# w_in's second piece as one transfer of 512 KB on SP's queue instead of two of 256 KB

## Chip, core and metric

The kernel runs on one core of a Trainium2 chip. The metric is the device time of one execution in microseconds. TensorE (PE) multiplies, with its weight loads listed apart (PEld); VectorE (DVE), ScalarE (ACT) and GpSimd (POOL) do the elementwise work; SP only issues transfers. SP and ScalarE each have a queue of transfers, and both queues are served by the same 16 DMA engines.

## What is computed

One input x (2048 rows of 512, bf16) goes through two mixers, and a gate per row mixes their outputs:

```python
g = _sigmoid((x * gate_w).sum(-1, keepdims=True))
a = _A_ref(x, A_wqkv, A_w_phi, A_wo)       # linear attention, 32 heads of 16
b = _B_ref(x, B_w_in, B_w_sp, B_b_sp, B_w_out)
return g * a + (1 - g) * b
```

The change lies in the loads of the second mixer's first weight, `B_w_in` (512 x 1376):

```python
z = _gelu(jnp.einsum('bsd,df->bsf', x, w_in))
z1 = z[..., :Fh].copy()
z2 = _layernorm(z[..., Fh:], axis=-1)
g = jnp.einsum('ts,bsf->btf', w_sp, z2) + b_sp[None, :, None]
return jnp.einsum('bsf,fd->bsd', z1 * g, w_out)
```

## The kernel before

The 2048 rows are 16 tiles of 128. Everything stays in SBUF; the order of the instructions on each engine is the order in which the program writes them, and a framework adds the semaphores. First comes z = x w_in for all tiles, with the projections for the attention woven in from tile 5 on, then the keys together with the spatial product with w_sp, then the queries and the output.

The tile `w_in` holds the weight as [128 partitions, 4 blocks of 128 rows (dt), 1376 + 1 columns]; the last column is the gate's weight, put there by a small matmul (line 209) and a copy on VectorE (line 212). The product of a tile t with it is made in three pieces of columns, `Z_PIECES`: 0 to 511, 512 to 1023 and 1024 to 1376. A piece is one matmul for each dt (line 180), added up in PSUM; then ScalarE takes the GELU (line 215).

Tiles 0 and 1 are treated apart, because the weight is still arriving. Their x comes as rows (`xn`) and is transposed by TensorE, which first spins on a constant (line 189). The first piece is cut into two halves of 256 columns, and within a piece the two tiles alternate, dt by dt. For the second piece that means eight matmuls in the order dt 0 tile 0, dt 0 tile 1, dt 1 tile 0 and so on. The third piece follows tile by tile, and after tile 1 comes tile 2 with all its pieces, which reads the first transposed load of x (`xT`, line 123).

The loads of the beginning are issued in this order. On SP's queue: rows 0 to 127 of x (128 KB), blocks 0 and 1 of the first piece's two halves (two of 128 KB), the second piece as blocks 0 and 1, then 2 and 3 (two of 256 KB, lines 118 and 119), the third piece (352 KB, line 122), the transposed load of tiles 2 and 3 (line 123), wv (512 KB, line 124), and then further transposed loads. On ScalarE's queue: rows 128 to 255 of x, blocks 2 and 3 of the first piece's halves (two of 128 KB), and the gate's weight.

The framework has eight completion semaphores for such transfers and hands them out in turn, over both queues. A transfer that gets a semaphore for the second time waits, on the queue that issues it, until the transfer that had it first has landed. The second half of the second piece is the ninth transfer in that count; it takes the semaphore of the load of x on ScalarE's queue. The copy of line 212 writes a column of `w_in` and waits for the transfers of the columns about it, the third piece's among them.

Of the kernel before, what the change touches and what calls it, by code (L numbers as in the profile page):

```python
# [23 lines left out]
NDT = D // P  # L24
CH = 512
# [14 lines left out]
def kernel(  # L40
# [14 lines left out]
    nc = tc.nc  # L55
# [55 lines left out]
    def load_w_in(eng, d0, d1, n0, n1):  # L111
        eng.dma_start(out=w_in[:, d0:d1, n0:n1], in_=w_in_v[:, d0:d1, n0:n1])

    HC = CH // 2
    for n0 in (0, HC):
        load_w_in(nc.sync, 0, 2, n0, n0 + HC)
        load_w_in(nc.scalar, 2, 4, n0, n0 + HC)
    for d0 in (0, 2):
        load_w_in(nc.sync, d0, d0 + 2, CH, 2 * CH)
    nc.scalar.dma_start(out=gw[:], in_=gate_w.rearrange("(dt p) -> dt p", p=P))  # L120
    nc.scalar.activation(out=st[:, 9, 0:1], in_=ones[:, 0:1], func=AF.Gelu_apprx_tanh)
    nc.sync.dma_start(out=w_in[:, :, 2 * CH:F], in_=w_in_v[:, :, 2 * CH:F])
# [451 lines left out]
```

## Time and profile before

| | us |
|---|---|
| median of 3 runs (lowest to highest) | 208.38 (208.34 to 208.63) |
| the profiled execution's own time | 208.87 |
| its span, first to last instruction | 207.1 |
| TensorE busy | 202.6 (98% of the span) |
| VectorE busy | 148.5 (72%) |
| ScalarE busy | 82.1 (40%) |
| GpSimd busy | 49.5 (24%) |

The profile is one execution of the program. Each engine's busy time is the time in which it had an instruction in work; matmuls overlap in the pipeline, so the eight 128x512 matmuls of a piece are listed with some 0.38 us each and start 0.22 us apart. The granted clock of TensorE is 1.0 throughout. A transfer has two times: that of its issue on the queue, and the time from the start of the issue to the landing, at which its semaphore is complete. The 16 DMA engines moved 26.5 MB in all, 128 GB/s over the span; in the first four of the span's 40 slices (5.2 us each) it was 188, 233, 188 and 255.

### The profile page before, as it was taken

To read this page: it belongs to the slowest core of one execution; us is meant where nothing else is said; L and a number is where in the kernel's file an instruction comes from. 1 tells how busy PE (TensorE), PEld (TensorE's weight loads), DVE (VectorE), ACT (ScalarE), POOL (GpSimd) and SP (SyncE) were. 2 spreads that over 40 slices of the span, in tenths; PEclk is the share of its full clock that TensorE was granted. 3 is DMA by queue.
4 is the path that set the end of the run, shared out by engine and by line. 5 is a ranking of instruction groups with operands and counts; after the bars stand their busy time and mean duration, and the time that the engine had idled before them with its cause. 6 is when DMAs were issued, how large, how long until landed. Compare 5 with 4: busy or idle time off the path is not lost.

```text
span 207.1 us, 3685 instructions
## 1 busy us (share of the span) xinstructions
PE 202.6 (98%) x1399; PEld 118.2 (57%) x1399; DVE 148.5 (72%) x304; ACT 82.1 (40%) x145; POOL 49.5 (24%) x46
## 2 busy tenths in 40 slices
PE   8899999999999999999999999999999999999994
PEld 7454555555455666666666667666455555555543
DVE  1048858376887988878888996698989778795500
ACT  3266757575684424250505102222524243341122
POOL 4000000000002343525352544032522252322000
DMA  6999899997000634472757771137765963567451
GB/s 188 233 188 255 178 178 227 173 188 234 0 3 0 138 69 112 101 127 67 162 118 112 139 170 41 38 90 76 170 140 119 151 162 80 134 135 164 101 104 51
DMA packets 90378, 26.50 MB, mean 128 GB/s; under 512 B 84168, under 2 KB 90360, under 8 KB 90360
## 3 DMA queue, kind: packets, MB, share of 16 engines
q1 hardware_dynamic: 87360, 23.84, 58.9%
q10 hardware_dynamic: 3000, 2.43, 3.9%
q8 instruction: 11, 0.18, 0.4%
q14 instruction: 7, 0.06, 0.1%
HBM read 3.44 MB, written 2.10 MB: 27 GB/s over the span
## 4 chain that ended last, share of the span: by engine, by line
PE 98%; issue 0%; ACT 0%; DVE 0%
PE ps L396 36%; PE ps L180 18%; PE ps L327 13%; PE ps L439 10%; PE ps L444 7%; PE ps L282 7%; PE ps L420 2%; PE ps L372 2%; PE ps L189 1%; PE ps L305 1%; PE ps L195 0%; ACT ob L448 0%; DVE w_in L212 0%; PE ps L209 0%
## 5 line engine op out<-in xcount | busy, mean ns | idle before, releaser
L396 PE MATMUL ps<-zz,wsp 128*128 128x344 bf16 x512 | 79.1, 310 | 0.0
L342 POOL TENSOR_TENSOR w_in<-w_in,rs 128x512 bf16<-128x512 bf16 x28 | 41.3, 1475 | 124.8 <-DVE rs L340 117.3
L396 PEld LDWEIGHTS <-wsp 128*128 128x128 bf16 x512 | 49.9, 98 | 27.9
L333 ACT ACTIVATE w_in<-ps 128x512 bf16<-128x512 f32 x56 | 30.1, 596 | 63.5 <-issue 21.5
L180 PE MATMUL ps<-w_in,xT 128*128 128x512 bf16 (+2 forms) x200 | 39.8, 350 | 0.7 <-DVE w_in L212 0.7
L338 DVE TENSOR_REDUCE zs<-w_in 128x64 f32<-128x1024 bf16 x28 | 33.8, 1209 | 0.0
L404 DVE SCALAR_TENSOR_TENSOR u<-ps,bcol,zz 128x344 bf16<-128x344 f32 x32 | 18.4, 574 | 18.6 <-PE ps L396 18.5
L180 PEld LDWEIGHTS <-xT 128*128 128x128 bf16 x200 | 18.9, 97 | 18.5 <-DMA w_in<-in_B_w_in_dram 1.0
L215 ACT ACTIVATE zz<-ps 128x1376 bf16<-128x1376 f32 (+2 forms) x18 | 21.4, 1190 | 18.9 <-PE ps L180 18.8
L439 PE MATMUL ps<-w_out,uT 128*128 128x512 bf16 (+1 forms) x102 | 23.5, 367 | 0.0
L224 DVE BATCH_NORM_STATS2 stats<-zz 128x6 f32<-128x344 bf16 x32 | 14.8, 505 | 11.2 <-ACT zz L215 11.2
L342 DVE TENSOR_TENSOR w_in<-w_in,rs 128x512 bf16<-128x512 bf16 x28 | 19.4, 692 | 1.0
L340 DVE RECIPROCAL rs<-zs 128x64 f32<-128x64 f32 x32 | 17.7, 552 | 3.2
L448 ACT ACTIVATE ob<-ps 128x512 bf16<-128x512 f32 (+1 forms) x17 | 9.7, 572 | 25.2 <-PE ps L444 23.7
L444 PE MATMUL ps<-wo,oT 128*128 128x512 bf16 (+1 forms) x68 | 16.6, 367 | 0.0
L327 PE MATMUL ps<-wq,xT 128*128 128x512 bf16 x64 | 16.4, 379 | 0.0
L327 PE MATMUL ps<-wk,xT 128*128 128x512 bf16 x64 | 16.2, 379 | 0.0
L327 PEld LDWEIGHTS <-xT 128*128 128x128 bf16 x128 | 10.8, 97 | 9.0
L282 PE MATMUL ps<-wv,xT 128*128 128x512 bf16 x64 | 15.6, 380 | 0.0
L439 PEld LDWEIGHTS <-uT 128*128 128x128 bf16 x102 | 9.7, 98 | 10.0
L426 DVE SCALAR_TENSOR_TENSOR o<-ps,st,rd 128x512 bf16<-128x512 f32 x16 | 12.0, 751 | 0.6
L444 PEld LDWEIGHTS <-oT 128*128 128x128 bf16 x68 | 6.7, 98 | 7.2
(56 smaller groups left out, 119.2 us busy)
## 6 DMA issues: line engine op xcount, KB each, us to landing
out_dram<-ob ACTq DMA_DIRECT2D x15, 128.0 KB, 1.9
w_out<-in_B_w_out_dram SPq DMA_DIRECT2D x1, 640.0 KB, 5.0
w_in<-in_B_w_in_dram SPq DMA_DIRECT2D x2, 256.0 KB, 4.1
wv<-in_A_wqkv_dram SPq DMA_DIRECT2D x1, 512.0 KB, 5.0
wo<-in_A_wo_dram SPq DMA_DIRECT2D x1, 512.0 KB, 5.4
w_in<-in_B_w_in_dram SPq DMA_DIRECT2D x1, 352.0 KB, 5.2
w_in<-in_B_w_in_dram ACTq DMA_DIRECT2D x2, 128.0 KB, 3.9
w_in<-in_B_w_in_dram SPq DMA_DIRECT2D x2, 128.0 KB, 3.5
```

The lines of the kernel that those rows point to most:

```text
L180: nc.tensor.matmul(zb[:, n0:n1], lhsT=xT[:, dt, t * P:(t + 1) * P], rhs=w_in[:, dt, n0:n1], start=(dt == 0), stop=(dt == NDT - 1),)
L215: nc.scalar.activation(out=zz[:, t, n0:n1], in_=zbank(t)[:, n0:n1], func=AF.Gelu_apprx_tanh)
L282: nc.tensor.matmul(ps[:, b, :], lhsT=xT[:, dt, t * P:(t + 1) * P], rhs=wv[:, dt, :], start=(dt == 0), stop=(dt == NDT - 1),)
L327: nc.tensor.matmul(ps[:, b, :], lhsT=xT[:, dt, t * P:(t + 1) * P], rhs=w[:, dt, :], start=(dt == 0), stop=(dt == NDT - 1),)
L333: nc.scalar.activation(out=e[:, :, a, :], in_=src, func=AF.Exp, scale=sc)
L338: nc.vector.tensor_reduce(out=zs[:], in_=ev, axis=AX.X, op=ALU.add)
L340: nc.vector.reciprocal(out=rs[:], in_=zs[:])
L342: eng.tensor_tensor(out=ev[:, sl, :], in0=ev[:, sl, :], in1=rs[:, sl, None].to_broadcast([P, H, DH]), op=ALU.mult,)
L396: nc.tensor.matmul(ps[:, b, 0:HF], lhsT=wsp[:, tt % WSLOTS, s, :], rhs=zz[:, s, FH + h * HF:FH + (h + 1) * HF], start=(s == 0), stop=(s == ...
L404: nc.vector.scalar_tensor_tensor(out=u[:, h * HF:(h + 1) * HF], in0=ps[:, b, 0:HF], scalar=bcol[:, tt:tt + 1], in1=zz[:, tt, h * HF:(h + 1 ...
L439: nc.tensor.matmul(ps[:, b, n0:n1], lhsT=uT[:, ft, :], rhs=w_out[:, ft, n0:n1], start=(ft == 0), stop=False,)
L444: nc.tensor.matmul(ps[:, b, n0:n1], lhsT=oT[:, g, :], rhs=wo[:, g, n0:n1], start=False, stop=(g == NDT - 1),)
```

## The change

The two transfers of the second piece, each with two of the four blocks, become one with all four. It brings the same bytes to the same place, with rows of 1024 bytes as before; the matmuls that read them are the same. There is one transfer less in the program, so each later one gets the semaphore before the one it had: the 512 KB are the eighth transfer, and the third piece is now the ninth. Every line number below moves up by one.

```diff
     for n0 in (0, HC):
         load_w_in(nc.sync, 0, 2, n0, n0 + HC)
         load_w_in(nc.scalar, 2, 4, n0, n0 + HC)
-    for d0 in (0, 2):
-        load_w_in(nc.sync, d0, d0 + 2, CH, 2 * CH)
+    load_w_in(nc.sync, 0, NDT, CH, 2 * CH)
     nc.scalar.dma_start(out=gw[:], in_=gate_w.rearrange("(dt p) -> dt p", p=P))
     nc.scalar.activation(out=st[:, 9, 0:1], in_=ones[:, 0:1], func=AF.Gelu_apprx_tanh)
     nc.sync.dma_start(out=w_in[:, :, 2 * CH:F], in_=w_in_v[:, :, 2 * CH:F])
```

## The prediction

> **What bounds the kernel now.** I read the page's chain of waits first, to see whose time the span is, then the same chain in order of time for the first microseconds, because the edit touches a load that is over before 10 us.
>
> ```profile
> PE 98%; issue 0%; ACT 0%; DVE 0%
> ```
>
> The span is TensorE's work, in a row. A load can change the time only where TensorE stands still for it. The chain in order of time (start us, us, what) shows one such place in the stretch of w_in:
>
> ```profile
> 4.93 1.98 PE ps L180 x15
> 6.91 0.11 PE ps L209
> 7.01 1.63 PE ps L180 x7
> 8.65 0.70 issue
> 9.35 0.19 DVE w_in L212
> 9.54 0.04 issue
> 9.58 10.69 PE ps L180 x56
> ```
>
> The matmuls of w_in's second piece (columns 512 to 1023) run from 6.95 to 8.65; then TensorE does nothing for 0.93 us; from 9.58 on it has no gap. The time line names what ended the gap (start us, us, engine, line; in brackets the idle time before):
>
> ```profile
> 6.95 1.90 PE L180 MATMUL ps<-w_in,xT 128*128 128x512 bf16 x8
> 9.31 0.10 PEld L180 LDWEIGHTS <-xT 128*128 128x128 bf16 x1 [0.96 <-DMA w_in<-in_B_w_in_dram]
> 9.35 0.17 DVE L212 CAST w_in<-ps 128x4 bf16<-128x4 f32 x1 [4.36 <-PE ps L180]
> 9.58 0.31 PE L180 MATMUL ps<-w_in,xT 128*128 128x353 bf16 x1 [0.73 <-DVE w_in L212]
> ```
>
> It is the landing of the third piece (line 122, 352 KB) at 9.31. VectorE's small copy of the gate column waits for the same landing, although its row names TensorE, whose product had been ready since 7.01; 0.27 us after the landing the first matmul of the third piece starts. So for the start of the gapless rest two things count: when the third piece lands, plus 0.27, and when TensorE is through with the second piece.
>
> The third view is SP's queue and what its transfers take (start and length of the issue; then KB and us from issue to landing, in order of issue: the two halves of the second piece, and the third piece):
>
> ```profile
> 2.23 0.47 SPq L112 DMA_DIRECT2D w_in<-in_B_w_in_dram  x1
> 3.69 0.37 SPq L112 DMA_DIRECT2D w_in<-in_B_w_in_dram  x1
> 4.11 0.47 SPq L122 DMA_DIRECT2D w_in<-in_B_w_in_dram  x1
> 4.62 2.23 SPq L123 DMA_TRANSPOSE xT<-in_A_x_dram  x1
> ```
>
> ```profile
> w_in<-in_B_w_in_dram SPq DMA_DIRECT2D x1, 256.0 KB, 4.4
> w_in<-in_B_w_in_dram SPq DMA_DIRECT2D x1, 256.0 KB, 3.8
> w_in<-in_B_w_in_dram SPq DMA_DIRECT2D x1, 352.0 KB, 5.2
> ```
>
> The first half lands at 2.23 + 4.4 = 6.63, the second at 3.69 + 3.8 = 7.5 (7.52 before rounding), the third piece at 4.11 + 5.2 = 9.31. Between 2.70 and 3.69 SP issues nothing, and its waits say why:
>
> ```profile
> SPq L112 <- DMA xn<-in_A_x_dram: 1.0, 1, 1.0
> ```
>
> In the built program there are eight completion semaphores in turn, so the ninth transfer, now the second half, waits until the first one (xn's, ScalarE's queue, 0.80 + 2.9 = 3.70) has landed.
>
> Last, whether the transfers are held up by their issue or by the DMA engines (window, its length, busy times, clock, DMA share, GB/s):
>
> ```profile
> 4.50:5.50 1.00, 1.00 (x12) 0.60 (x11) 0.49 (x2) 0.72 (x3) 0.00 (x0) 1.00 1.11 342
> 5.50:6.50 1.00, 1.00 (x10) 0.75 (x8) 0.00 (x0) 0.00 (x0) 0.00 (x0) 1.00 0.92 236
> 6.50:7.50 1.00, 1.00 (x8) 0.51 (x7) 0.00 (x0) 0.60 (x1) 0.00 (x0) 1.00 1.26 299
> ```
>
> The engines are busy throughout, so a transfer issued sooner mostly stands longer in the queue. But the rate falls from 342 to 236 GB/s after 5.5, just when the late-issued half and third piece have their turn.
>
> **The change, part by part.** *What goes on SP.* One of two issues goes, one of twice the size stays. The wv load has the same 512 KB in the same four blocks and takes 0.57 us to issue, against 0.47 + 0.37 now. In the changed program this transfer is the eighth and waits for nothing: issued at about 2.7, over by 3.3. The wait for xn moves to the third piece, so that this one is issued at 3.69 in place of 4.11, 0.42 sooner. Queued behind it on SP are the transposes of xT, the load of wv and all later ones, which move up by at most the same 0.42; TensorE shows no gap for any of them after 9.58, so that gives nothing. Their nearest margin is the first transpose (line 123): it lands at 4.62 + 5.7 = 10.32 and is needed by tile 2, whose matmuls begin at 10.78. It follows the third piece in the queue and moves with it, so the 0.46 stays.
>
> *What goes on TensorE.* No matmul is added or removed. Today the second piece starts at 6.95, on the half landed at 6.63, and its fifth matmul (dt = 2) at 7.82, on the half landed at 7.52. After the change its first matmul needs both. The bytes, their order by piece and the engines are the same, so I take 7.52 for the landing of the whole. With 0.05 from release to matmul (the copy above ends at 9.53, the matmul starts at 9.58) it begins at 7.57, and with eight at the pitch of now (6.95 to 8.68, 1.73) the third piece could start at 9.30. That is 0.62 late for TensorE and still 0.28 before 9.58: the idle time is moved ahead of the second piece, not lengthened. ScalarE's GELU of the second piece moves from 8.67 to about 9.3 and, at 0.60 us, is over at 9.9, before the third piece's at 10.38.
>
> *What goes on the DMA engines.* How much sooner than 9.31 the third piece lands is not in the trace. From below: no sooner, since the engines are busy and 1 completion write in each engine is all that is saved. From above: by 0.42 as its issue does, or by the stall. The trace's records of single packets hold, from 5.6 to 7.4 us, some 16 packets (one for each engine on the average) that last 0.16 to 0.92 us where their neighbours last 0.03 to 0.05, 7.1 us in all, 0.44 an engine. I take zero: the DMA share is 0.92 to 1.26 in these windows, and the first packets of a transfer show some 1.3 us after its issue begins (xn: 0.80 and 2.13), so that the second half stood ready at about 5.0, before the first engine was through with the first half (5.2).
>
> *The sum* for the profiled execution: 0.00, with 0.28 to spare; its span of 207.1 and time of 208.87 stay. The timed runs have a median of 208.38, 0.49 less. Where that lies isn't shown. If it lies in the third piece, which would land there at 8.82 and free TensorE at 9.09, the second piece's end at 9.30 would come last: +0.21. I take the middle, +0.1, and forecast 208.5.
>
> **The rivals.** *The queue is filled in time (faster).* If the long packets come from the second half's late issue, 0.44 goes: the whole second piece lands at 7.08 and is through at 8.86, the third lands at 8.87 or sooner and starts at 9.14 at the latest. That is 0.44 less, 207.9; where the third lands still sooner, the second piece's end at 8.86 is the floor, 0.72 less, 207.7. For it speaks that the rate falls where the late transfers run; against it the busy engines, and that some of the long packets belong to the third piece, which was issued right behind.
>
> *The lost overlap (slower).* Now four matmuls run on the first half while the second is on its way. In one transfer, the slowest of 16 engines holds up all eight. It decides once the 512 KB land later than 9.31 + 0.27 - 0.05 - 1.73 = 7.80, 0.28 after the 7.52 that I took. An engine can be that late: of the third piece's 16 completion writes 15 stand before 8.43 and the last at 9.13, 0.70 later. The same in the second piece gives 8.22, the end of its matmuls 10.00 and 0.42 more; where the third piece isn't late itself (8.82, above) 0.91 more. So 208.6 to 209.3, and 208.9 in the middle. Against it stands that both halves' own slowest engines were through by 7.52.
>
> For this rival the Trainium skill has a rule (Perfetto Trace Analysis, DMA Optimizations): splitting a DMA lets parts start sooner, above all where the DMA engines are idle. Here they aren't, as the share above shows, so by the rule's own condition little is lost by joining. The skill also says that a transfer counts as landed only when all the engines it uses have written their completion (DMA: Bandwidth & Descriptors, "Why a DMA increments its semaphore by 16 and not by 1"); the 16 writes of the third piece, the last 0.70 behind, agree.
>
> **How the numbers follow.** About 0.2% (0.42 us) is what a measurement of this kernel can tell from no change. The forecast, in which the gap only moves, has 0.38, with a range of its own of 208.2 to 208.7, all of it within 0.2%. Faster by the filled queue has 0.28, of it 0.23 beyond 0.2%. Slower by the lost overlap has 0.34, more than the filled queue because the margin of 0.28 is the smaller of the two quantities and the timed runs may have less; 0.30 of it is beyond 0.2%. That gives 0.23 faster, 0.47 same (0.38 + 0.05 + 0.04) and 0.30 slower. The range of 207.7 to 209.2 reaches from the floor of the faster rival to just below the far end of the slower one.
>
> **What would show it.** In the profile after: SP's issues of the second piece at 2.70, with no wait behind them until the third piece's at 3.69; TensorE idle from about 6.9 to 7.6, the eight 128x512 matmuls of line 179 packed until 9.3; a gap of 0.3 or less in front of the third piece, whose first matmul starts at 9.4 to 9.6; from there on the same gapless row. A landing of the 512 KB after 7.8 shows the lost overlap, landings of it near 7.1 and of the third piece below 8.9 the filled queue. A gap of TensorE after 10 us that isn't there now would make the whole reading wrong.

## Result and profile after

| | before | after |
|---|---|---|
| median of 6 runs, us (lowest to highest) | 208.36 (208.30 to 208.63) | 209.26 (209.06 to 209.50) |
| profiled execution, us | 208.87 | 209.16 |
| its span, us | 207.1 | 207.4 |

The change makes the kernel slower: ratio 1.0043, 95% interval 1.0032 to 1.0054, or 0.90 us by the medians. The prediction was 208.5, with 209.2 as its upper end. The two profiled executions differ by 0.29 only: the one before took 0.51 more than its median, the one after 0.10 less than its own.

The chain of waits of the kernel after, by engine, has a new entry, the landing of w_in:

```profile
PE 95%; DMA 3%; SPq 1%; ACT 0%; issue 0%
```

In order of time (start us, us, what) it shows where:

```profile
2.23 5.78 DMA w_in<-in_B_w_in_dram
8.01 0.04 issue
8.05 12.42 PE ps L179 x64
```

The 512 KB land at 8.01; the second piece starts at 8.05, and from there TensorE has no gap. The 0.9 us of waiting ahead of the third piece are gone altogether. TensorE's time line shows two waits ahead of that:

```profile
6.93 0.60 PE L179 MATMUL ps<-w_in,xT 128*128 128x256 bf16 x4 [0.58 <-DMA w_in<-in_B_w_in_dram]
7.46 0.17 PE L208 MATMUL ps<-ident,gw 4*128 4x4 bf16 x1
8.05 0.38 PE L179 MATMUL ps<-w_in,xT 128*128 128x512 bf16 x1 [0.41 <-DMA w_in<-in_B_w_in_dram]
```

The last four matmuls of the first piece wait until 6.93, which they did not before: there the first piece was over at 6.91. What they wait for is in the list of transfers (KB, us from issue to landing; in order, the second piece from 2.23, ScalarE's second 128 KB from 1.73, the third piece from 3.72):

```profile
w_in<-in_B_w_in_dram SPq DMA_DIRECT2D x1, 512.0 KB, 5.8
w_in<-in_B_w_in_dram ACTq DMA_DIRECT2D x1, 128.0 KB, 5.2
w_in<-in_B_w_in_dram SPq DMA_DIRECT2D x1, 352.0 KB, 5.4
```

ScalarE's second 128 KB, blocks 2 and 3 of the first piece, took 4.5 before and 5.2 now (in a second pair of profiles, below, it is 5.1 before and 4.5 after). SP's queue itself went as forecast, with the wait moved to the third piece:

```profile
3.72 0.37 SPq L121 DMA_DIRECT2D w_in<-in_B_w_in_dram  x1
4.14 2.54 SPq L122 DMA_TRANSPOSE xT<-in_A_x_dram  x1
```

The windows that fell in rate after 5.5 before now have the low rate one microsecond sooner (last column GB/s):

```profile
4.50:5.50 1.00, 1.00 (x11) 0.70 (x10) 0.53 (x3) 0.72 (x3) 0.00 (x0) 1.00 0.95 266
5.50:6.50 1.00, 0.85 (x8) 0.61 (x8) 0.00 (x0) 0.00 (x0) 0.00 (x0) 1.00 0.98 317
6.50:7.50 1.00, 0.57 (x5) 0.33 (x4) 0.00 (x0) 0.04 (x1) 0.00 (x0) 1.00 1.06 336
```

### The profile page after: what moved, and what is told of

It reads as the page before. It is cut to its first block, busy times and chain, and to the rows that moved or that the text cites. A ratio compares the mean times of both kernels' runs of the same rounds, so it can differ in the third digit from the quotient of the medians.

```text
span 207.4 us, 3682 instructions
## 1 busy us (share of the span) xinstructions
PE 202.5 (98%) x1399; PEld 118.4 (57%) x1399; DVE 148.6 (72%) x304; ACT 82.1 (40%) x145; POOL 49.2 (24%) x46
## 4 chain that ended last, share of the span: by engine, by line
PE 95%; DMA 3%; SPq 1%; ACT 0%; issue 0%
PE ps L395 36%; PE ps L179 17%; PE ps L326 13%; PE ps L438 10%; PE ps L443 7%; PE ps L281 7%; DMA w_in<-in_B_w_in_dram 3%; PE ps L419 2%; PE ps L371 2%; PE ps L304 1%; SPq L112 0%; SPq L108 0%; ACT ob L447 0%
```

## Experiments

The diffs show the lines that matter; the declarations of `gx` (tiles that nobody reads) and the changed head of `z_piece` are left out, and a few comments are added.

Theories: **O**, the overlap of the first half's matmuls with the second half's landing was lost. **Q**, the early issue of the second piece holds up ScalarE's transfers. **T**, an early transposed load does that. **E2** and **E3** came last: the low rate belongs to the early second piece, or to the early third piece. Each time below is the median, with the ratio to the kernel before, measured beside it, and its interval.

**A second profile of both kernels.** First the kernel before, unchanged.

> The kernel before, unchanged, for a second profile: the profiled execution shown of it took 208.87, 0.5 more than its median. Theory O, with the third piece's slowest DMA engine late in that one execution: a profile near 208.4 whose third piece lands near 8.8 and whose TensorE starts it near 9.1. Theory Q says nothing on this; the landing may stay at 9.3 and the 0.5 lie elsewhere.

Measured: 208.42, ratio 1.0002 (0.9994 to 1.0011); profiled execution 208.55. Its chain:

```profile
1.73 5.12 DMA w_in<-in_B_w_in_dram
6.85 0.04 issue
6.89 0.60 PE ps L180 x4
7.49 0.11 PE ps L209
7.59 4.55 PE ps L180 x23
```

There is no gap ahead of the third piece. It lands at 4.08 + 4.9 = 8.98, while TensorE is still in the second piece (7.53 to 9.26). What the row waits for here is ScalarE's second 128 KB at 6.85, by way of the first piece. So the landing at 9.31 that the prediction built on was that execution's.

> The changed kernel once more, for a second profile and more times: 209.0 to 209.5. Theory O: its gapless row starts about 0.9 later than that of the kernel before, with the 512 KB's landing as what it waited for. Theory Q: the row's start waits for ScalarE's second 128 KB first of all.

Measured: 209.16, ratio 1.0032 (1.0020 to 1.0045); profiled execution 208.89. The chain again has the 512 KB, landed at 7.76:

```profile
2.23 5.53 DMA w_in<-in_B_w_in_dram
7.76 0.04 issue
7.81 4.39 PE ps L179 x22
```

ScalarE's second 128 KB took 4.5 here and decided nothing; the 512 KB alone do.

**One account for all profiles.** Take the start of the gapless row, at the second piece's first matmul (where the third piece made TensorE wait, that matmul's start less the second piece's 1.73). The profiled execution's time less that start is the same within 0.2 in all:

| kernel | row start | time | difference |
|---|---|---|---|
| before | 9.58 - 1.73 = 7.85 | 208.87 | 201.02 |
| before, again | 7.53 | 208.55 | 201.02 |
| control, gw on GpSimd | 7.25 | 208.33 | 201.08 |
| late half first | 7.59 | 208.58 | 200.99 |
| after | 8.05 | 209.16 | 201.11 |
| after, again | 7.81 | 208.89 | 201.08 |
| joined, late | 8.22 | 209.21 | 200.99 |
| two early halves | 8.16 | 209.33 | 201.17 |

The other eight profiles give 200.91 to 201.14. So the row's start is the whole effect; by it the medians of 208.36 and 209.26 mean starts near 7.3 and 8.2 (an estimate). Of the profiles with the old loads or the control's, the control's is the nearest to the median, and in it no load decides: the first piece's matmuls start 0.21 us apart until 5.93 and 0.11 apart after it, where the first profile before has 0.11 nearly throughout. So TensorE's pace at the start differs between executions too; what sets it is not shown.

**The lost overlap by itself.** The loads of before; TensorE takes the late half first.

```diff
-        for dt in range(NDT):
-            z_piece(0, n0, n1, dt, dt + 1)
-            z_piece(1, n0, n1, dt, dt + 1)
+        o = (2, 3, 0, 1) if n0 == CH else (0, 1, 2, 3)
+        for dt in o:
+            z_piece(0, n0, n1, dt, dt + 1, o[0], o[-1])   # start at o[0], stop at o[-1]
+            z_piece(1, n0, n1, dt, dt + 1, o[0], o[-1])
```

> The loads are those of the kernel before, two transfers of 256 KB; only TensorE's order in the second piece of tiles 0 and 1 is changed, to dt 2, 3, 0, 1, so that its first matmul needs the half that lands last. Theory O (the overlap of the first half's matmuls with the second half's landing is what was lost): the second piece starts near 7.55 in place of 6.95 and ends near 9.3, and the time rises to 208.6 to 209.0. Theory Q (the larger transfer, standing in SP's queue 1 us sooner, holds up ScalarE's transfers and so everything): no change, 208.3 to 208.5.

Measured: 208.72, ratio 1.0019 (1.0011 to 1.0028). The chain:

```profile
3.83 3.71 DMA w_in<-in_B_w_in_dram
7.55 0.04 issue
7.59 4.61 PE ps L180 x23
```

With no transfer changed, waiting for the later half costs about 0.4 us. Theory O holds, for something less than half of the 0.9.

**Two halves, both early.** The gate's weight goes to GpSimd's queue, so that the second half is the eighth transfer and doesn't wait.

```diff
-    nc.scalar.dma_start(out=gw[:], in_=gate_w.rearrange("(dt p) -> dt p", p=P))
+    nc.gpsimd.dma_start(out=gw[:], in_=gate_w.rearrange("(dt p) -> dt p", p=P))
```

> Two transfers of 256 KB as before, but the gate's weight is loaded on GpSimd's queue, so that the second half is the eighth transfer and is issued at about 2.7 without a wait, and the third piece at about 3.7. Theory O: no slower than before, 208.0 to 208.4, the first half's matmuls running ahead of the second half's landing. Theory Q: ScalarE's second 128 KB land near 6.9 in place of 6.2, as after the change, and the time is 208.9 to 209.3 in spite of the two halves.

Measured: 208.81, ratio 1.0017 (1.0008 to 1.0026). Slower than before though nothing is joined, against theory O alone. In the profile ScalarE's second 128 KB, issued at 1.74, land at 7.49 and decide; but this execution, of 209.33, is the slowest of the eleven, so what decides in a usual one is not shown:

```profile
1.74 5.75 DMA w_in<-in_B_w_in_dram
7.49 0.04 issue
7.53 0.60 PE ps L180 x4
```

The control has the gate's weight on GpSimd's queue as well, and a transfer of 1 KB in its old place.

```diff
-    nc.scalar.dma_start(out=gw[:], in_=gate_w.rearrange("(dt p) -> dt p", p=P))
+    nc.gpsimd.dma_start(out=gw[:], in_=gate_w.rearrange("(dt p) -> dt p", p=P))
+    nc.scalar.dma_start(out=gx[:], in_=gate_w.rearrange("(dt p) -> dt p", p=P))
```

> A control for the kernel with two early halves: the gate's weight comes on GpSimd's queue as there, but a transfer of the same 1 KB into an unread tile keeps its place on ScalarE's queue, so that the second half is the ninth transfer again and is issued at 3.7. Theory O and theory Q: 208.2 to 208.5, no change against the kernel before. If the move to GpSimd's queue is what cost 0.2% there, 208.6 to 208.9.

Measured: 208.35, ratio 1.0001 (0.9992 to 1.0010). The move to GpSimd's queue costs nothing that shows; the early issue does.

**One transfer that nobody waits for in the second piece.**

```diff
-                zb[:, n0:n1], lhsT=xT[:, dt, t * P:(t + 1) * P], rhs=w_in[:, dt, n0:n1],
+                zb[:, n0:n1], lhsT=xT[:, dt, t * P:(t + 1) * P], rhs=w_in[:, dt, n0 - sh:n1 - sh],
...
-            z_piece(0, n0, n1, dt, dt + 1)
-            z_piece(1, n0, n1, dt, dt + 1)
+            z_piece(0, n0, n1, dt, dt + 1, CH if n0 == CH else 0)   # sh
+            z_piece(1, n0, n1, dt, dt + 1, CH if n0 == CH else 0)
```

> The changed kernel with its one transfer of 512 KB, but in tiles 0 and 1 the eight matmuls of the second piece multiply by the first piece's columns, so that they need nothing of the 512 KB (their products are not the reference's; all the rest of the work is there). Theory O: the wait for the 512 KB goes, the second piece starts as soon as the first is through, near 7.5, and the time falls to 208.3 to 208.7. Theory Q: the larger transfer still stands in SP's queue early and ScalarE's second 128 KB still land late; of the 0.9 lost at least 0.4 stays, 208.7 to 209.1. Both: in between, 208.5 to 208.9.

Measured: 209.03, ratio 1.0021 (1.0008 to 1.0034). In the profile, of the slowest execution of seven (209.18), ScalarE's second 128 KB land at 7.42 and decide the first piece's end; the second starts at 8.10:

```profile
1.74 5.68 DMA w_in<-in_B_w_in_dram
```

Without the wait for the 512 KB the same 0.2% is left as with two early halves. So the loss has two parts, 0.19% from the wait and 0.17 to 0.21% from the early issue, together 0.36 to 0.40% against 0.43% (0.32 to 0.54) and 0.32% (0.20 to 0.45) measured for the change. That each part costs something is clear of the noise; the shares are not sharp, since the interval here (0.08 to 0.34%) meets that of the change itself.

**Both issues late.** A transfer of 1 KB on SP makes the second piece wait for the first load of x.

```diff
+    nc.sync.dma_start(out=gx[:], in_=gate_w.rearrange("(dt p) -> dt p", p=P))
     load_w_in(nc.sync, 0, NDT, CH, 2 * CH)
```

> One transfer of 512 KB, but a transfer of 1 KB (the gate's weight once more, into a tile that nobody reads) stands before it on SP, so that the 512 KB are the ninth and are issued at 3.7, when the second half was issued before the change. Theory O: as slow as after the change or a little slower, 209.0 to 209.6. Theory Q: ScalarE's second 128 KB land near 6.2 again, and most of the loss is gone, 208.4 to 208.8.

Measured: 209.73, ratio 1.0066 (1.0050 to 1.0082). The chain (the 512 KB issued at 3.49):

```profile
3.49 4.70 DMA w_in<-in_B_w_in_dram
8.18 0.04 issue
8.22 3.96 PE ps L181 x20
```

ScalarE's 128 KB came early, 3.8 after their issue, and the first piece was over at 6.5; TensorE then stood 1.62 us for the 512 KB. The same with two halves:

```diff
+    nc.sync.dma_start(out=gx[:], in_=gate_w.rearrange("(dt p) -> dt p", p=P))
     for d0 in (0, 2):
         load_w_in(nc.sync, d0, d0 + 2, CH, 2 * CH)
```

> Two transfers of 256 KB, both late: a transfer of 1 KB before them on SP makes the first half the ninth transfer, so that the halves are issued at about 3.5 and 3.9, as the 512 KB were in the joined kernel with the same 1 KB. Against that one only the number of transfers differs. Theory O: the first half's matmuls run while the second half comes, so it is 0.4 to 0.9 below the joined one's 209.7, 208.8 to 209.3. Theory Q: with the same late issue there is little between them, 209.4 to 209.8.

Measured: 208.62, ratio 1.0010 (1.0000 to 1.0020). Below what O had forecast: with a late issue, splitting is worth 0.56%, 1.1 us by the medians.

**What takes the rate.** In the window from 4.5 to 5.0 the kernels fall in two groups. With the second half held back until the first load of x has landed, it was 354 and 318 GB/s (before, twice), 364 (late half first), 327 (control) and 351 (quarters, below, whose last two are held back in the same way); with the whole second piece issued at once, 248 and 227 (after, twice), 201 (two early halves) and 232 (not needed). From 4.5 to 5.5, the microsecond that the expectations name, the same kernels have 305 to 350 and 242 to 267. The transposed load of tiles 2 and 3 moves up too, so it was held back alone:

```diff
     nc.sync.dma_start(out=w_in[:, :, 2 * CH:F], in_=w_in_v[:, :, 2 * CH:F])
+    for g in gx:                                  # two tiles that nobody reads
+        nc.sync.dma_start(out=g[:], in_=gate_w.rearrange("(dt p) -> dt p", p=P))
     nc.sync.dma_start_transpose(out=xT[:, :, 2 * P:CH], in_=x2[2 * P:CH, :])
```

> The changed kernel, with two transfers of 1 KB (into unread tiles) between the third piece and the transposed load of tiles 2 and 3 on SP, so that the transposed load is issued at about 4.9 in place of 4.0 to 4.1; the 512 KB and the third piece are issued as after the change. Theory T (the DMA engines lose rate about 0.5 to 1.9 us after a transposed load is issued, and the change moves that stretch from the second piece onto ScalarE's second 128 KB): the rate from 4.5 to 5.5 is back at 330 to 350 GB/s from 242 to 285, ScalarE's second 128 KB land at 5.8 to 6.3, and the time is 208.6 to 208.9, the wait for the whole 512 KB being left. Theory Q (the early 512 KB themselves hold up ScalarE's transfers): no change, 209.0 to 209.4. Theory O alone: no change either.

Measured: 208.80, ratio 1.0021 (1.0010 to 1.0032), with the 512 KB landed at 8.01. The window (277 GB/s from 4.5 to 5.5, where T expected 330 to 350):

```profile
4.50:5.00 0.50, 0.50 (x6) 0.40 (x5) 0.41 (x2) 0.49 (x3) 0.00 (x0) 1.00 1.05 259
```

The same edit on the kernel with two early halves:

> Two early halves, the gate's weight on GpSimd's queue, and the same two transfers of 1 KB ahead of the transposed load of tiles 2 and 3, which is issued at about 4.8 in place of 4.0. Theory T: the loss of 0.2% of the two early halves goes, 208.0 to 208.4, with ScalarE's second 128 KB landing near 6. Theory Q: it stays, 208.6 to 208.9.

Measured: 208.45, ratio 1.0014 (1.0001 to 1.0028); 253 GB/s in that window (283 over the microsecond), ScalarE's second 128 KB 5.7 after their issue, in a profile of the slowest execution of twelve (209.42). The first time lies in T's range and the second between T's and Q's, but not by T's way: the rate stays low. T falls. Whether holding the load back helps at all is not clear, since the intervals meet those without it.

The same two transfers ahead of the third piece hold that one back, with one transfer of 512 KB in the first kernel and with two early halves in the second.

```diff
+    for g in gx:
+        nc.sync.dma_start(out=g[:], in_=gate_w.rearrange("(dt p) -> dt p", p=P))
     nc.sync.dma_start(out=w_in[:, :, 2 * CH:F], in_=w_in_v[:, :, 2 * CH:F])
```

> The changed kernel with two transfers of 1 KB (into unread tiles) before the third piece on SP, so that the third piece is issued at about 4.5 in place of 3.6 and the transposed load at about 5.0; the 512 KB stay at 2.2 to 2.7. Theory E3 (the low rate from 4.0 to 5.5 us comes with the early third piece): the rate from 4.5 to 5.5 is 320 to 350 GB/s, and the time 208.5 to 208.9. Theory E2 (it comes with the second piece's early issue): the rate stays at 240 to 290, and the time at 208.8 to 209.3.

Measured: 208.77, ratio 1.0016 (1.0004 to 1.0027). The time lies in E3's range, just below E2's; the rate is E2's, 249 GB/s from 4.5 to 5.5. The interval lies below that of the change's first measurement and meets that of its second, so whether this helps is open too. The window:

```profile
4.50:5.00 0.50, 0.50 (x7) 0.27 (x5) 0.50 (x3) 0.33 (x3) 0.00 (x0) 1.00 0.87 195
```

> Two early halves with the gate's weight on GpSimd's queue, and the same two transfers of 1 KB before the third piece, which is issued at about 4.5 in place of 3.6. Theory E3: 320 to 350 GB/s from 4.5 to 5.5 and 208.0 to 208.4. Theory E2: 240 to 290 GB/s and 208.4 to 208.9.

Measured: 208.49, ratio 1.0016 (1.0000 to 1.0031); 249 GB/s from 4.5 to 5.0, though 309 over the whole microsecond that the expectation named. The time is E2's; 309 fits neither. From 4.5 to 5.0 the low rate is there in every kernel that issues the second piece at once, with the third piece early or late: E2, by a window that no expectation had named. (The two kernels with both issues late have 124 and 142 GB/s in that window for another reason, their second piece having been issued only from 3.5 to 3.8 on.)

The low rate is not a loss of bytes. From 5.5 to 7.5 the kernels with the early second piece moved 302 to 356 GB/s and the five others 267 to 328, and from 1.5 to 8.0 the means are 262 to 274 and 261 to 276. So by 8.0 as much had arrived either way, and that the low rate is what costs the time is not shown: ScalarE's second 128 KB landed at 6.85 in the second profile before, at 318 GB/s, and at 6.21 in the second after, at 227. So Q is right that the early issue costs something, but not shown to be right in its way. What moves with the early issue is the landing of single transfers. The first half of the second piece is issued at 2.23 to 2.25 in eight of the profiles. It took 4.2 to 5.0 us in the four with the second half held back, and 4.5 to 5.8 in the four with it early, two of which show a kernel's slowest execution.

**Other ways to share the load.**

```diff
-    for d0 in (0, 2):
-        load_w_in(nc.sync, d0, d0 + 2, CH, 2 * CH)
-    nc.scalar.dma_start(out=gw[:], in_=gate_w.rearrange("(dt p) -> dt p", p=P))
+    load_w_in(nc.sync, 0, 2, CH, 2 * CH)
+    load_w_in(nc.scalar, 2, 4, CH, 2 * CH)
+    nc.gpsimd.dma_start(out=gw[:], in_=gate_w.rearrange("(dt p) -> dt p", p=P))
```

> The second piece's blocks 0 and 1 on SP's queue and 2 and 3 on ScalarE's, behind its own first-piece loads, the gate's weight on GpSimd's queue. Neither queue is deeper than the other, and the transposed load of tiles 2 and 3 is issued at about 4.1. Theory Q: nothing holds up ScalarE's second 128 KB, 208.0 to 208.4. Theory T: the early transposed load still takes rate from 4.5 to 5.5, 208.5 to 208.9.

Measured: 208.86, ratio 1.0031 (1.0020 to 1.0043); 256 GB/s from 4.5 to 5.0. ScalarE's second 128 KB were no later than before (4.4), but the first piece still ended at 7.5:

```profile
4.69 2.78 PE L180 MATMUL ps<-w_in,xT 128*128 128x256 bf16 x16
```

That is not a load's doing: no wait stands in this row, and its matmuls start 0.21 us apart until 6.40 and 0.11 apart after that. The second piece starts at 7.59, when its first half has landed (2.24 + 5.3). So the early issue costs, and the low rate comes, from either queue: it isn't SP's queue being the deeper one.

```diff
-    for d0 in (0, 2):
-        load_w_in(nc.sync, d0, d0 + 2, CH, 2 * CH)
+    for d0 in range(NDT):
+        load_w_in(nc.sync, d0, d0 + 1, CH, 2 * CH)
```

> The second piece in four transfers of 128 KB, one for each dt, on SP's queue. Theory O: each pair of matmuls waits for its own quarter, so the second piece isn't late; but the third piece is issued some 0.8 later than before, at about 4.9, and the transposed load at 5.4; if the third piece then lands at 9.6 to 9.8, as with the two late halves, its wait decides: 208.5 to 208.9. Theory T: with the transposed load that late ScalarE's second 128 KB land at 5.8 to 6.2.

Measured: 208.74, ratio 1.0030 (1.0016 to 1.0043). As expected the second piece starts in time, at 7.11, and the third piece, issued at 4.93 and landed at 9.05, makes TensorE wait until 9.40. ScalarE's second 128 KB landed at 6.09, as T had it, but they had landed at 6.27 before and at 5.87 with the late half first too. None of these kernels beats the kernel before.

## Why the prediction was wrong

*That TensorE's first gapless row sets the time: right.* Time less row start is 200.9 to 201.2 in every profile, and none shows a new gap after 10 us. The moved wait on SP, the third piece at 3.72, the end of the gap ahead of it and the packed second piece all came. One detail was off: the 512 KB take the place of the first half and were issued at 2.23, not at 2.7.

*The landing of the 512 KB: the step that failed, a term too small.* Taken as 7.52, it was 8.01 and 7.76, and a row start near 8.2 in the medians means a landing near 8.15 (an estimate). "The bytes, their order by piece and the engines are the same" left out two things: that one transfer is released only with its slowest engine, and that the earlier issue costs something by itself (0.17%). In the packet records of the first profile after, 13 of the 16 completion writes that by their order are the 512 KB's stand within 0.50 us, and the next comes 0.67 later; the last of its packets of 1024 bytes starts at 7.54, 0.94 after the thirteenth write. Those are the slowest engines, as in the slower rival.

*The margin of 0.28: the second step that failed.* It rested on the third piece's landing at 9.31 in one execution. In three other profiles with these or the control's loads it lands at 8.98 (before), 8.48 (control) and 8.75 (late half first), where nothing waits for it. There was no gap to absorb the delay. The prediction had seen the sign of this, 0.49 between the profiled execution and the median, and gave it half its weight as +0.1. By its own sum the full weight gives +0.21, so 208.6, still within its range; the other 0.7 of the way to 209.26 is the late landing.

*The end of the first piece: kept at 6.91, but not steady.* In the first profile after, the gate's product, which follows it, starts at 7.46 in place of 6.84, because ScalarE's second 128 KB came 0.6 later. In the second pair it is the other way about, 7.42 before and 7.20 after. So no delay of the first piece by the change is shown; two profiles of one kernel differ by as much.

*The times of single packets* in the prediction lie 0.3 us late against the views: the first packet of xn is at 1.82, not 2.13. The differences between them, the 0.70 above all, stand.

*The rivals.* The lost overlap was right in kind: waiting for the whole costs 0.19% by itself, and 0.56% with a late issue. That its "0.91 more" meets the measured 0.90 is in part luck, since it was priced on the slowest engine alone and about half of the loss goes with the early issue. How the early issue delays the landings is open. The filled queue didn't come: the early issue brought the low rate forward, and by 8.0 us no more had arrived.

*The rule on splitting* (the Trainium skill, Perfetto Trace Analysis, DMA Optimizations) was read by its condition, idle DMA engines, as speaking for little loss. The engines were busy, with a share of 0.91 to 1.26 in the windows of before and late half first from 4.5 to 7.5, and the wait for the later half still cost 0.19% there; with the late issue, at a share of 0.70 to 1.08, splitting was worth 0.56%. What counts here is who waits, not whether the engines are idle.

## What to carry to other kernels

A load that matmuls take in order can be worth splitting along that order even when the DMA engines are busy, as here, because each part's own completion is what releases work. Ask of a transfer issued sooner what is in flight beside it that is needed first: 256 KB issued 0.8 us sooner, with what follows them, cost 0.17% here. A gap of some tenths of a microsecond in one profiled execution that is half a microsecond over the median is no margin: take a second profile, or price the change with the gap closed. A landing read from one profile is a sample too; the third piece landed at 8.48 to 9.31 with the same loads or the control's.

## What was not expected of the hardware

Filling a queue sooner brought a stretch of low rate forward. With the whole second piece issued at once, from SP or from both queues, the DMA engines moved 195 to 259 GB/s from 4.5 to 5.0 us; with its second half held back they moved 318 to 364, all with data queued. By 8.0 us the bytes were the same. In the first pair of profiles the packets of the two queues that last 0.15 us or more fit that: from 4.0 to 5.0 us two start before and six after, from 5.6 to 7.5 fifteen before and three after. What in the engines does this is open: neither the transposed load nor the third piece behind it made the difference, and the depth of the queue itself wasn't varied alone.

What comes late in a late transfer is its last packets. By 5.0 us ScalarE's queue had moved 0.38 MB of 0.39 in the first profile before and 0.37 in the first after, yet its second 128 KB landed 0.6 apart.
